# A two-dimensional FFT filter on one core: sequence length 2048 split 64 by 32 in place of 128 by 16

## The chip, the core and the metric

The kernel runs on one NeuronCore of a Trainium2 chip. TensorE (PE) multiplies matrices and writes PSUM. ScalarE (ACT) and VectorE (DVE) work on elements and copy PSUM to SBUF. GpSimd (POOL) and SyncE (SP) issue DMA transfers here, and 16 DMA engines carry them. The metric is the device time of one execution in microseconds; smaller is better.

## The reference

Two filters act on the same input x of 2048 rows (s) by 1024 columns (d), in bf16. Each multiplies the real 2-D spectrum by a complex weight, and a gate for each row blends the two results:

```python
def reference(A_x, A_w_r, A_w_i, B_x, B_w_r, B_w_i, gate_w):
    x = A_x
    g = sigmoid((x * gate_w).sum(-1, keepdims=True))
    a = irfft2(rfft2(x.astype(float32)) * (A_w_r + 1j * A_w_i), s=(2048, 1024)).astype(bfloat16)
    b = irfft2(rfft2(x.astype(float32)) * (B_w_r + 1j * B_w_i), s=(2048, 1024)).astype(bfloat16)
    return g * a + (1 - g) * b
```

The input B_x is not used.

## The kernel before

All transforms are matmuls with constant matrices (`make_constants`, lines 49 to 125). A row index is written s = 16 s2 + s1: s2 (128 values) lies on the SBUF partitions and s1 (16 values) along them. The transform over s is done in two steps, 128 by 16. The transform over d is split into even frequencies (`par` 0, with 257 columns) and odd ones (`par` 1, with 256). Frequencies of s come in 16 tiles t, and two tiles are a unit; there are 8 units for each parity, so n runs from 0 to 15, the even ones first.

1. First forward step (lines 214 to 228). For each s1, 8 matmuls with F1 contract s2 and fold d with d + 512; ScalarE and VectorE in turn copy the result into y.
2. Unit steps, for each n. f2 (8 matmuls with FD, L275, copy into T, L279) contracts d. f3 (12 matmuls of 64x64 tiles with WF, L295, in parity 0 also 8 of one column, L303; copy into X, L310) does the s1 step of the forward transform. cmul (four VectorE operations, L325 to L331) multiplies by the weights of A and B. i1 (two rounds r of 8 matmuls with WI, L344, copy into rl, L349) does the first inverse step over s. After the second round POOL issues the exchange (L354): the rows of rl, which have frequency and s1 on the partitions, go to RR[par], where 128 components of s2 lie on the partitions and s1 lies along them.
3. Output blocks, for each parity and v from 0 to 7, with two values of s1 in a block. i2 (L367, 16 pairs of weight load and matmul of 128 columns) contracts the 128 components of A with the tile EA and then those of B with EB, adding both in PSUM; ScalarE copies the result into V (L370). i3 (L378, 8 matmuls of 512 columns with IG) does the inverse over d. For parity 0 the result is kept in SBUF in fp32, copied by ScalarE for v below 3 (L384) and by VectorE after that (L386). For parity 1 VectorE forms the sum and the difference (L389, L390) and SP stores both halves of d.

The gate is computed from the same spectrum. `gate_hat` contracts y with the gate weight, ScalarE writes zs with single elements moved apart (L245), and a small transfer on ScalarE's queue (L246) puts one logit component on each partition (zt). `gate_z` (L254) multiplies zt, repeated over 128 columns, with Ez, so that the logit stands on every partition, and ScalarE applies the sigmoid (L256). `gate_weights(b)` forms EA = g E (L261) and EB = E - EA (L262) for four values of s1.

The order is written out by hand (lines 393 to 449) and every engine keeps it. Unit steps are staggered: in round n stand f2(n), i1(n-3, 0), f3(n-1), i1(n-3, 1), cmul(n-1). From n = 12 on, i2(0, v) and i3(0, v) stand between the unit steps of the odd parity: i2(0, 0) follows i1(9, 1). The last i2 of parity 0 and all of parity 1 follow the last unit. The PSUM pool pt has three buffers; the i2 result pv has one (`bufs=1`, L413), so an i2 waits for the copy of the one before it. The buffers rl are four: the copy for unit n + 4 waits for the exchange of unit n. RR[0] takes the place of x, RR[1] that of weight tiles, and the fp32 tile EV shares the bytes of RR[0]. POOL's transfers use eight completion semaphores in turn, so that in the built program each transfer also waits until the eighth one before it has landed. SP issues the loads of x, of the constants and of the weights in the order of lines 163 to 201, and the later weight loads from within the rounds.

Of the kernel before, what the change touches and what calls it, by code (L numbers as in the profile page):

```python
# [27 lines left out]

def quad_reps(t):
    return (0, 32, 16, 48) if t == 0 else (t, t + 32, t + 64, t + 96)  # L30


def half_k2(t, jh):
    a, b = quad_reps(t)[2 * jh:2 * jh + 2]
    if t == 0 and jh == 0:
        return (0, 64, 32, 96)
    return (a, 128 - a, b, 128 - b)


def half_rows(t, jh):  # L40
    return np.array([k2 + 128 * k1 for k2 in half_k2(t, jh) for k1 in range(16)])

# [6 lines left out]
def make_constants():  # L49
    c = {}  # L50
    s2 = np.arange(128)
    F = np.zeros((128, NT, 2, 2, 2))
    E = np.zeros((NT, 2, 2, 2, 128))
    EZ = np.zeros((NT, 2, 2, 2, 128))
    for t in range(NT):
        for j, k2 in enumerate(quad_reps(t)):
            th = 2 * np.pi * s2 * k2 / 128
            F[:, t, j // 2, 0, j % 2] = np.cos(th)
            F[:, t, j // 2, 1, j % 2] = -np.sin(th)
            E[t, j // 2, 0, j % 2] = np.cos(th)  # L60
            E[t, j // 2, 1, j % 2] = np.sin(th)
            EZ[t, j // 2, 0, j % 2] = 2 * np.cos(th)
            EZ[t, j // 2, 1, j % 2] = -2 * np.sin(th)
            if k2 == 0:
                F[:, t, j // 2, 1, j % 2] = np.cos(np.pi * s2)
                E[t, j // 2, 1, j % 2] = np.cos(np.pi * s2)
                EZ[t, j // 2, 0, j % 2] = 1
                EZ[t, j // 2, 1, j % 2] = np.cos(np.pi * s2)
# [24 lines left out]
    c["IG"] = _bf16np(IG.reshape(2, 2, 2, 128, 512).transpose(3, 0, 1, 2, 4).reshape(128, 8, 512))  # L93
    s1 = np.arange(NS1)
    WF = np.zeros((128, NT, 3, 64))
    WI = np.zeros((128, NT, 3, 64))
    for t in range(NT):
        for jh in range(2):
            k = half_rows(t, jh)
            reps = quad_reps(t)[2 * jh:2 * jh + 2]  # L100
            al = np.zeros((NS1, 2, 2, 64), dtype=complex)
            be = np.zeros((2, 2, NS1, 64), dtype=complex)
            for p in range(64):
                w = np.exp(-2j * np.pi * k[p] * s1 / S)
                kk = k[p] % 128
                if kk in (0, 64):
                    cc = 0 if kk == 0 else 1
                    al[:, cc, 0, p] = w
                    be[cc, 0, :, p] = w.conj()
                    continue  # L110
                eps = 1 if kk in reps else -1
                j = reps.index(kk if eps > 0 else 128 - kk)
                al[:, 0, j, p] = w
                al[:, 1, j, p] = 1j * eps * w
                be[0, j, :, p] = w.conj()
                be[1, j, :, p] = 1j * eps * w.conj()
            al = al.reshape(64, 64)
            be = be.reshape(64, 64).T
# [10 lines left out]
def gated_mix(ctx, tc, x_in, we_in, wo_in, gw_in, out):  # L129
# [99 lines left out]

    RR = [r[:].rearrange("p (s f) -> p s f", s=NS1) for r in (Re, Ro)]  # L230
# [16 lines left out]

    g = const.tile([P, NS1, 128], BF16, name="g")

    def gate_z():  # L250
        for hh in range(2):
            ps = ptile()
            for s in range(8):
                nc.tensor.matmul(ps[:, s * 128:(s + 1) * 128], lhsT=zt[:, 8 * hh + s:8 * hh + s + 1].to_broadcast([P, 128]),  # L254
                                 rhs=Ez[:], start=True, stop=True)
            nc.scalar.activation(g[:, 8 * hh:8 * hh + 8, :].rearrange("p a b -> p (a b)"), ps[:], ACT.Sigmoid)  # L256

    def gate_weights(b):
        s = slice(4 * b, 4 * b + 4)
        e = bc(Ec[:]).to_broadcast([P, 4, 128])  # L260
        nc.vector.tensor_tensor(EA[:, s], g[:, s], e, ALU.mult)  # L261
        nc.vector.tensor_tensor(EB[:, s], e, EA[:, s], ALU.subtract)  # L262

# [70 lines left out]
    def i1(n, r):  # L334
        par, u = n // NU, n % NU
        Y = Ys[n]
        o = 1 if par == 0 and r == 1 else 0
        ps = ptile()
        for k in range(2):
            w = ((0, 2), (1, 0))[r][k]  # L340
            for tt in range(2):
                for jh in range(2):
                    hin = hp(jh ^ tt)
                    nc.tensor.matmul(ps[hp(jh), tt * 512:(tt + 1) * 512], lhsT=WI[hin, 2 * u + tt, w, :],  # L344
                                     rhs=Y[hin, k, 2 * tt:2 * tt + 2, o:o + 256], start=(k == 0), stop=(k == 1))
        if r == 0:
            RLs[n] = wk.tile([P, 2, 2, 512], BF16, name="rl", tag="rl", bufs=4)
        rl = RLs[n]
        nc.scalar.copy(out=rl[:, :, r, :], in_=ps[:].rearrange("p (t m) -> p t m", t=2))  # L349
        if r == 1:  # L350
            for tt in range(2):
                t = 2 * u + tt
                p0 = 32 * (t // 4) + t % 4
                nc.gpsimd.dma_start(RR[par][p0:p0 + 29:4, :, :], rl[:, tt].rearrange("p r m -> p (r m)"))  # L354
            RLs.pop(n), Ys.pop(n)
# [3 lines left out]
    def i2(par, v):  # L359
        ps = pq["p"].tile([P, 1024], F32, name="pv", tag="pv")  # L360
        V = wk.tile([P, 2, 4, 128], BF16, name="V", tag="V")
        for s in range(2):
            s1 = 2 * v + s
            for ch in range(4):
                c0 = (ch // 2) * 512 + (ch % 2) * 128
                for ab, Ew in enumerate((EA, EB)):
                    nc.tensor.matmul(ps[:, s * 512 + ch * 128:s * 512 + ch * 128 + 128],  # L367
                                     lhsT=RR[par][:, s1, c0 + 256 * ab:c0 + 256 * ab + 128], rhs=Ew[:, s1, :],
                                     start=(ab == 0), stop=(ab == 1))
        nc.scalar.copy(out=V[:].rearrange("p s c k -> p (s c k)"), in_=ps[:])  # L370
        Vs[par, v] = V
# [115 lines left out]
```

## Time and profile before

| what | value |
|---|---|
| time, median of 3 runs | 147.13 us (145.34, 147.13, 148.02) |
| profiled execution: span from first to last instruction | 144.4 us |
| profiled execution: its own device time | not given apart from the span |
| PE busy | 121.9 us, 1188 matmuls |
| DVE busy | 97.6 us, 113 instructions |
| ACT busy | 93.3 us, 97 instructions |
| POOL busy | 19.6 us, of which 32 exchange issues 19.1 us |
| DMA | 29.19 MB in 11088 packets, mean 202 GB/s |
| exchange alone | 8.41 MB in 4608 packets on POOL's queue |
| granted TensorE clock, mean | 0.961 of full speed |

A PE that is busy is not one at its peak, since matmuls overlap in the pipeline and each record holds its whole passage: a matmul of 128 columns is recorded with 219 ns, but the next one starts 56 ns later. Starts tell the pace. In a chain view each piece has its start, its length and the work that the next piece waited for.

### The profile page before, as it was taken

How to read it: one execution, taken by the hardware profiler on the slowest of the kernel's cores; microseconds unless marked ns; L12 is line 12 of the kernel's file. 1: busy time of each engine (PE TensorE's matmuls, PEld its weight loads, DVE VectorE, ACT ScalarE, POOL GpSimd, SP SyncE). 2: the span in 40 equal slices, each digit the busy share in tenths (PEclk: the TensorE clock that was granted, in tenths of full speed). 3: DMA queues.
4: the chain of work that ended last, by engine and by line, in shares of the span. 5: the costliest groups of instructions: out<-in, count | busy, mean ns of one | idle time of the engine just before them, and what ended most of it. 6: DMA issues, size and time to landing. Idle time of an engine off the chain costs nothing.

```text
span 144.4 us, 2878 instructions
## 1 busy us (share of the span) xinstructions
PE 121.9 (84%) x1188; PEld 68.1 (47%) x1206; DVE 97.6 (68%) x113; ACT 93.3 (65%) x97; POOL 19.6 (14%) x37
## 2 busy tenths in 40 slices
PE   6999979929899898888867999868869999999910
PEld 2688844416344443334324345433455665756500
DVE  0177740089279999999999279599433456898990
ACT  4255546665699999999995899997935244253200
POOL 1000000000033222233333033033330000000000
PEclk9999999975799999999999999999999999999985
DMA  4999999968716999999865315527464000464553
GB/s 148 298 361 419 406 411 405 415 244 284 297 14 168 240 279 278 353 250 202 163 139 133 126 18 140 131 43 168 110 166 110 0 0 0 167 253 166 208 228 145
DMA packets 11088, 29.19 MB, mean 202 GB/s; under 512 B 3781, under 2 KB 4165, under 8 KB 10949
## 3 DMA queue, kind: packets, MB, share of 16 engines
q1 hardware_dynamic: 6048, 20.55, 38.3%
q0 software_dynamic: 4608, 8.41, 24.8%
q8 instruction: 9, 0.15, 0.5%
q10 hardware_dynamic: 420, 0.07, 0.3%
q14 instruction: 3, 0.02, 0.0%
HBM read 16.42 MB, written 4.19 MB: 143 GB/s over the span
## 4 chain that ended last, share of the span: by engine, by line
PE 55%; ACT 24%; DMA 9%; issue 4%; DVE 2%; another core or an unknown queue 2%; DVEq 1%; POOL 0%; ACTq 0%; POOLq 0%
PE pt L378 18%; PE pt L218 10%; PE pt L275 10%; ACT rl L349 10%; PE pv L367 9%; DMA re<-rl 5%; DMA zt<-zs 4%; ACT X L310 4%; ACT T L279 3%; PE pt L344 3%; ACT V L370 2%; PE pt L155 2%; ACT zs L245 2%; DVE ot L390 2%
## 5 line engine op out<-in xcount | busy, mean ns | idle before, releaser
L275 PE MATMUL pt<-fd,y 128*128 128x512 bf16 x117 | 30.5, 394 | 3.8 <-ACT rl L349 2.6
L349 ACT CAST rl<-pt 128x1024 bf16<-128x1024 f32 x32 | 32.9, 1038 | 0.0
L378 PE MATMUL pt<-ig,V 128*128 128x512 bf16 x121 | 29.6, 379 | 1.1 <-ACT V L370 0.7
L370 ACT CAST V<-pv 128x1024 bf16<-128x1024 f32 x16 | 16.3, 1021 | 19.2 <-PE pv L367 19.2
L344 PE MATMUL pt<-Y,wi 64*64 64x512 bf16 x256 | 20.1, 387 | 3.8 <-ACT T L279 0.8
L275 PEld LDWEIGHTS <-y 128*128 128x128 bf16 x128 | 12.6, 100 | 20.3 <-issue 8.6
L279 ACT CAST T<-pt 128x1024 bf16<-128x1024 f32 x16 | 16.3, 1017 | 8.3 <-PE pt L275 4.1
L378 PEld LDWEIGHTS <-V 128*128 128x128 bf16 x128 | 11.7, 98 | 13.9 <-ACT V L370 1.9
L354 POOL DMA_DIRECT2D re<-rl x16 | 9.6, 606 | 59.8 <-ACT rl L349 59.8
L310 ACT CAST X<-pt 128x1024 bf16<-128x1024 f32 x16 | 16.5, 1033 | 0.0
L218 PE MATMUL pt<-f_84,re 128*128 128x256 bf16 x128 | 15.6, 289 | 0.0
L218 PEld LDWEIGHTS <-re 128*128 128x128 bf16 x128 | 13.0, 103 | 3.1 <-DMA re<-in_x_dram 0.8
L228 ACT CAST y<-pt 128x1024 bf16<-128x1024 f32 x8 | 8.1, 1013 | 8.4 <-PE pt L218 8.4
L354 POOL DMA_DIRECT2D ro<-rl x16 | 9.5, 596 | 26.4 <-ACT rl L349 26.4
L386 DVE COPY re<-pt 128x1024 f32<-128x1024 f32 x5 | 6.1, 1225 | 10.2 <-PE pt L378 10.2
L226 DVE CAST y<-pt 128x1024 bf16<-128x1024 f32 x7 | 8.6, 1225 | 5.2 <-PE pt L218 5.2
L344 PEld LDWEIGHTS <-wi 64*64 64x64 bf16 x256 | 6.4, 106 | 11.9 <-issue 10.7
L389 DVE TENSOR_TENSOR ot<-pt,re 128x1024 bf16<-128x1024 f32 x8 | 9.8, 1224 | 3.0 <-PE pt L378 3.0
L367 PE MATMUL pv<-ea,re 128*128 128x128 bf16 x64 | 8.1, 219 | 2.9 <-DMA re<-rl 1.7
L295 PE MATMUL pt<-T,wf 64*64 64x512 bf16 (+2 forms) x192 | 9.8, 307 | 0.4 <-ACT T L279 0.3
L367 PEld LDWEIGHTS <-re 128*128 128x128 bf16 x128 | 7.5, 98 | 5.4 <-issue 2.5
L390 DVE TENSOR_TENSOR ot<-re,pt 128x1024 bf16<-128x1024 f32 x8 | 9.7, 1210 | 0.0
(96 smaller groups left out, 128.2 us busy)
## 6 DMA issues: line engine op xcount, KB each, us to landing
re<-rl POOLq DMA_DIRECT2D x16, 256.0 KB, 8.0
ro<-rl POOLq DMA_DIRECT2D x16, 256.0 KB, 5.1
out_dram<-ot SPq DMA_DIRECT2D x8, 512.0 KB, 2.6
re<-in_x_dram SPq DMA_DIRECT2D x7, 512.0 KB, 8.6
ro<-in_we_dram SPq DMA_DIRECT2D x4, 516.0 KB, 8.0
y<-in_wo_dram SPq DMA_DIRECT2D x4, 512.0 KB, 6.5
fd<-cst_fd SPq DMA_DIRECT2D x2, 512.0 KB, 9.1
ig<-cst_ig SPq DMA_DIRECT2D x1, 1024.0 KB
```

What stands on the lines that cost most here:

```text
L218: nc.tensor.matmul(ps[:, q * 256:(q + 1) * 256], lhsT=x[:, s1, h * 512 + q * 128:h * 512 + (q + 1) * 128], rhs=(bc(F1[:, 0, :]).to_broadca ...
L275: nc.tensor.matmul(ps[:, tt * 512:(tt + 1) * 512], lhsT=y[:, q, par, 2 * t:2 * t + 2, :, :].rearrange("p j s c -> p (j s c)"), rhs=FD[:, p ...
L279: nc.scalar.copy(out=T[:].rearrange("p a b -> p (a b)"), in_=ps[:])
L295: nc.tensor.matmul(ps[ho, tt * 512 + dst:tt * 512 + dst + ln], lhsT=WF[hp(jh), 2 * u + tt, w, :], rhs=T[hp(jh), tt, src:src + ln], start=( ...
L310: nc.scalar.copy(out=xo, in_=ps[:].rearrange("p (t r m) -> p t r m", t=2, r=2))
L344: nc.tensor.matmul(ps[hp(jh), tt * 512:(tt + 1) * 512], lhsT=WI[hin, 2 * u + tt, w, :], rhs=Y[hin, k, 2 * tt:2 * tt + 2, o:o + 256], start ...
L349: nc.scalar.copy(out=rl[:, :, r, :], in_=ps[:].rearrange("p (t m) -> p t m", t=2))
L354: nc.gpsimd.dma_start(RR[par][p0:p0 + 29:4, :, :], rl[:, tt].rearrange("p r m -> p (r m)"))
L367: nc.tensor.matmul(ps[:, s * 512 + ch * 128:s * 512 + ch * 128 + 128], lhsT=RR[par][:, s1, c0 + 256 * ab:c0 + 256 * ab + 128], rhs=Ew[:, s ...
L370: nc.scalar.copy(out=V[:].rearrange("p s c k -> p (s c k)"), in_=ps[:])
L378: nc.tensor.matmul(ps[:, s * 512:(s + 1) * 512], lhsT=V[:, s, ch, :], rhs=IG[:, par * 4 + ch, :], start=(ch == 0), stop=(ch == 3))
L390: nc.vector.tensor_tensor(ot[:, :, 1, :], ev, pv, ALU.subtract)
```

## The change

A row index is now split 64 by 32. The partitions still hold s2 = 0 to 127 with s = 16 s2 + s1, but the matrices read s2 as 2 p + h: p (64 values) is the long part, and s1 + 16 h (32 values) the short one. A tile's 128 rows are now four frequencies of 64 with 32 steps each, where they were eight of 128 with 16.

- The A and B components, 64 each, lie together on the 128 partitions of RR: A on 0 to 63, B on 64 to 127. One matmul contracts both, with a single tile EG: E times sigmoid(z) on partitions 0 to 63 and E times sigmoid(-z) on 64 to 127. The sign is a scale operand (sgn, two POOL memsets) of the sigmoid. i2 keeps 16 matmuls, each now with 64 columns and no accumulation.
- `gate_weights` is one VectorE operation on 8 x 64 elements in place of two on 4 x 128; EA and EB are one tile EG.
- The copy into V puts the two halves h next to each other: it reads PSUM in order and writes with a step of two elements.
- The exchange of a unit is four transfers, one for each tile and each of A and B: 4 partitions of 32 pieces of 1 KB, where two transfers had 8 partitions of 16 pieces of 2 KB. The copy into rl writes runs of 256 elements, not 512.
- `gate_z` has 32 matmuls of 64 rows and 64 columns in place of 16 of 128 and 128. Ez and Ec are smaller, and zt has 64 partitions of 32 elements instead of 128 of 16.

Everything else stays, the number of matmuls in the other stages and the written order included. In the changed file the lines stand some 6 lines earlier: the exchange is at L348, i2's matmul at L361, the copy into rl at L344.

```diff
-    Ec = const.tile([P, 128], BF16, name="ec")
-    Ez = const.tile([P, 128], BF16, name="ez")
+    Ec = const.tile([P, 64], BF16, name="ec")
+    Ez = const.tile([64, 64], BF16, name="ez")
...
-    EA = const.tile([P, NS1, 128], BF16, name="ea")
-    EB = const.tile([P, NS1, 128], BF16, name="eb")
-    zt = const.tile([P, NS1], BF16, name="zt")
+    EG = const.tile([P, 32, 64], BF16, name="eg")
+    zt = const.tile([64, 32], BF16, name="zt")
+    sgn = const.tile([P, 1], F32, name="sgn")
+    nc.gpsimd.memset(sgn[0:64], 1.0)
+    nc.gpsimd.memset(sgn[64:128], -1.0)
...
-            for s in range(8):
-                nc.tensor.matmul(ps[:, s * 128:(s + 1) * 128], lhsT=zt[:, 8 * hh + s:8 * hh + s + 1].to_broadcast([P, 128]),
+            for i in range(16):
+                w, sp = divmod(16 * hh + i, 2)
+                s1 = w + 16 * sp
+                nc.tensor.matmul(ps[:, i * 64:(i + 1) * 64], lhsT=zt[:, s1:s1 + 1].to_broadcast([64, 128]),
                                  rhs=Ez[:], start=True, stop=True)
-            nc.scalar.activation(g[:, 8 * hh:8 * hh + 8, :].rearrange("p a b -> p (a b)"), ps[:], ACT.Sigmoid)
+            nc.scalar.activation(g[:, 16 * hh:16 * hh + 16, :].rearrange("p a b -> p (a b)"), ps[:], ACT.Sigmoid, scale=sgn[:])
...
     def gate_weights(b):
-        s = slice(4 * b, 4 * b + 4)
-        e = bc(Ec[:]).to_broadcast([P, 4, 128])
-        nc.vector.tensor_tensor(EA[:, s], g[:, s], e, ALU.mult)
-        nc.vector.tensor_tensor(EB[:, s], e, EA[:, s], ALU.subtract)
+        s = slice(8 * b, 8 * b + 8)
+        nc.vector.tensor_tensor(EG[:, s], g[:, s], bc(Ec[:]).to_broadcast([P, 8, 64]), ALU.mult)
...
-            RLs[n] = wk.tile([P, 2, 2, 512], BF16, name="rl", tag="rl", bufs=4)
+            RLs[n] = wk.tile([P, 4, 2, 256], BF16, name="rl", tag="rl", bufs=4)
         rl = RLs[n]
-        nc.scalar.copy(out=rl[:, :, r, :], in_=ps[:].rearrange("p (t m) -> p t m", t=2))
+        nc.scalar.copy(out=rl[:, :, r, :], in_=ps[:].rearrange("p (t m) -> p t m", t=4))
         if r == 1:
-            for tt in range(2):
-                t = 2 * u + tt
-                p0 = 32 * (t // 4) + t % 4
-                nc.gpsimd.dma_start(RR[par][p0:p0 + 29:4, :, :], rl[:, tt].rearrange("p r m -> p (r m)"))
+            for ta in range(4):
+                p0 = 64 * (ta % 2) + 16 * (ta // 2) + u % 4 + 32 * (u // 4)
+                nc.gpsimd.dma_start(RR[par][p0:p0 + 13:4, :, :], rl[:, ta].rearrange("p r m -> p (r m)"))
...
         for s in range(2):
-            s1 = 2 * v + s
             for ch in range(4):
-                c0 = (ch // 2) * 512 + (ch % 2) * 128
-                for ab, Ew in enumerate((EA, EB)):
-                    nc.tensor.matmul(ps[:, s * 512 + ch * 128:s * 512 + ch * 128 + 128],
-                                     lhsT=RR[par][:, s1, c0 + 256 * ab:c0 + 256 * ab + 128], rhs=Ew[:, s1, :],
-                                     start=(ab == 0), stop=(ab == 1))
-        nc.scalar.copy(out=V[:].rearrange("p s c k -> p (s c k)"), in_=ps[:])
+                for sp in range(2):
+                    k = 4 * v + 2 * s + sp
+                    nc.tensor.matmul(ps[:, s * 512 + ch * 128 + sp * 64:s * 512 + ch * 128 + sp * 64 + 64],
+                                     lhsT=RR[par][:, k, ch * 128:ch * 128 + 128], rhs=EG[:, k, :], start=True, stop=True)
+        nc.scalar.copy(out=V[:].rearrange("p s c (k e) -> p (s c) e k", e=2), in_=ps[:].rearrange("p (a e k) -> p a e k", e=2, k=64))
```

Left out of the diff are the new contents of the constant matrices (F1, E, EZ, WF, WI), which change in value and not in the work that they cost, and RR's view as 32 by 512.

More of the change, by code (lines that the diff above doesn't have):

```diff
@@ L26, in _bf16np, with comp_row @@
     return np.ascontiguousarray(np.asarray(a, dtype=np.float32).astype(ml_dtypes.bfloat16))
-def quad_reps(t):
-    return (0, 32, 16, 48) if t == 0 else (t, t + 32, t + 64, t + 96)
 def half_k2(t, jh):
[L34 to L37, printed above, removed]
+    b = 2 * t + jh
+    return (0, 32) if b == 0 else (b, 64 - b)
 def half_rows(t, jh):
-    return np.array([k2 + 128 * k1 for k2 in half_k2(t, jh) for k1 in range(16)])
+    return np.array([k2 + 64 * k1 for k2 in half_k2(t, jh) for k1 in range(32)])
+def comp_row(ab, b, cc):
+    t, jh = b // 2, b % 2
+    u, tt = t // 2, t % 2
+    return 64 * ab + 16 * tt + 4 * (2 * jh + cc) + u % 4 + 32 * (u // 4)
 def unit_rows(t):
@@ L50, in make_constants @@
     c = {}
[L51 to L68, printed above, removed]
+    s2 = np.arange(64)
+    F = np.zeros((64, 2, 32, 2, 2))
+    E = np.zeros((128, 64))
+    EZ = np.zeros((32, 2, 64))
+    for b in range(32):
+        th = 2 * np.pi * s2 * b / 64
+        f = [np.cos(th), -np.sin(th)]
+        e = [np.cos(th), np.sin(th)]
+        ez = [2 * np.cos(th), -2 * np.sin(th)]
+        if b == 0:
+            f[1] = e[1] = ez[1] = np.cos(np.pi * s2)
+            ez[0] = np.ones(64)
+        for cc in range(2):
+            EZ[b, cc] = ez[cc]
+            for h in range(2):
+                F[:, h, b, cc, h] = f[cc]
+                E[comp_row(h, b, cc)] = e[cc]
     F = F.reshape(128, 128)
     c["F1"] = _bf16np(np.concatenate([F, -F], axis=1))
-    c["E"] = _bf16np(E.reshape(4, 4, 8, 128).transpose(0, 2, 1, 3).reshape(128, 128))
-    c["EZ"] = _bf16np(EZ.reshape(128, 128) / 128)
+    c["E"] = _bf16np(E)
+    c["EZ"] = _bf16np(EZ.reshape(64, 64) / 64)
     d1 = np.arange(512)
@@ L93, in make_constants @@
     c["IG"] = _bf16np(IG.reshape(2, 2, 2, 128, 512).transpose(3, 0, 1, 2, 4).reshape(128, 8, 512))
-    s1 = np.arange(NS1)
+    s1 = np.arange(32)
+    pos = np.array([w + 16 * sp for w in range(16) for sp in range(2)])
     WF = np.zeros((128, NT, 3, 64))
@@ L99, in make_constants @@
             k = half_rows(t, jh)
[L100 to L118, printed above, removed]
+            w = np.exp(-2j * np.pi * np.outer(s1, k) / S)
+            al = np.zeros((2, 32, 64), dtype=complex)
+            if t == 0 and jh == 0:
+                al[0, :, :32] = w[:, :32]
+                al[1, :, 32:] = w[:, 32:]
+                be = al.conj()
+            else:
+                eps = np.where(np.arange(64) < 32, 1, -1)
+                al[0], al[1] = w, 1j * eps * w
+                be = np.stack([w.conj(), 1j * eps * w.conj()])
+            al = al.reshape(2, 2, 16, 64).transpose(2, 0, 1, 3).reshape(64, 64)
+            be = be[:, pos].reshape(64, 64).T
             h = slice(64 * jh, 64 * jh + 64)
@@ L228, in gated_mix @@
             nc.scalar.copy(out=yo[:, :, s1, :], in_=i_)
[L230 removed]
+    RR = [r[:].rearrange("p (s f) -> p s f", s=32) for r in (Re, Ro)]
     EV = Re[:].bitcast(F32).rearrange("p (s f) -> p s f", s=NS1)
[L232 to L234 removed]
+    EG = const.tile([P, 32, 64], BF16, name="eg")
[3 more added lines that the diff above has]
+    nc.gpsimd.memset(sgn[64:128], -1.0)
     def gate_hat():
@@ L246, in gate_hat @@
         nc.scalar.dma_start(zt[:], zs[0:97:32].rearrange("p t c s -> p (t c s)"))
-    g = const.tile([P, NS1, 128], BF16, name="g")
+    g = const.tile([P, 32, 64], BF16, name="g")
     def gate_z():
```

## The prediction

> **What bounds the kernel now.** I read four views in this order: the busy time by stretches, the chain of work that ended last, single groups and stretches of the timeline where the chain passes an edited line, and the exchange transfers. The first says which engine limits each stage.
>
> ```profile
> core 0: us, PE busy (x) PEld busy (x) DVE busy (x) ACT busy (x) POOL busy (x), PEclk, DMA share, GB/s
> 0.80:37.50 36.70, 32.03 (x255) 20.59 (x262) 17.58 (x22) 19.14 (x19) 0.25 (x1) 0.91 0.93 348
> 37.50:74.90 37.40, 32.96 (x395) 15.10 (x400) 33.17 (x41) 35.57 (x38) 10.81 (x18) 1.00 0.83 214
> 74.90:104.90 30.00, 25.46 (x260) 12.37 (x266) 22.00 (x30) 26.41 (x29) 7.10 (x12) 1.00 0.44 108
> 104.90:120.30 15.40, 14.14 (x138) 9.41 (x139) 6.12 (x5) 6.08 (x7) 1.18 (x2) 1.00 0.24 64
> 120.30:144.40 24.10, 17.33 (x150) 10.62 (x150) 18.72 (x16) 6.07 (x6) 0.00 (x0) 0.91 0.43 175
> ```
>
> After the first columns (stretch, its length) stand the busy times. Until 37.5 us loads fill the DMA engines (0.93). From 37.5 to 74.9 ScalarE is full (35.57 of 37.40). From 74.9 to 104.9 ScalarE and TensorE alternate. From 104.9 TensorE carries the end, with VectorE close behind from 120.3.
>
> ```profile
> 69.90 6.53 DMA re<-rl
> ...
> 76.57 1.13 PE pv L367 x16
> ...
> 112.48 0.89 PE pv L367 x16
> 113.38 1.73 PE pt L378 x8
> ```
>
> In the chain (start, length, work) the last exchange transfer of the even half lands at 76.43 and releases the first i2 at 76.57. Later i2 (L367, 0.89) and i3 (L378, 1.73) alternate with no gap: one output block costs 2.62 us.
>
> ```profile
> 75.77 0.42 DVE L261 TENSOR_TENSOR ea<-g,ec 128x512 bf16<-128x512 bf16 x1
> 76.22 0.42 DVE L262 TENSOR_TENSOR eb<-ec,ea 128x512 bf16<-128x512 bf16 x1
> ...
> 136.10 1.23 DVE L389 TENSOR_TENSOR ot<-pt,re 128x1024 bf16<-128x1024 f32 x1 [0.27 <-PE pt L378]
> 137.24 1.21 DVE L390 TENSOR_TENSOR ot<-re,pt 128x1024 bf16<-128x1024 f32 x1
> 138.37 1.22 DVE L389 TENSOR_TENSOR ot<-pt,re 128x1024 bf16<-128x1024 f32 x1
> ```
>
> VectorE finishes the first gate tiles at 76.64, 0.2 us after that transfer: two waits end together at the first i2. At the end a pair of output operations needs 138.37 - 136.10 = 2.27 us, so VectorE has 0.35 us of air in each 2.62.
>
> ```profile
> L354 POOL DMA_DIRECT2D re<-rl x16: 596/596/745, 41.6 to 69.9; - x16
> DMA to landing us min/median/max: 4.5/8.0/12.0
> ```
>
> An issue costs POOL 0.596 us; even-half transfers landed 4.5 to 12.0 us after issue. The odd half's, with fewer loads beside them, took 4.3 to 5.7, median 5.1.
>
> **The change part by part.** *Second inverse stage, TensorE.* Each i2 keeps 16 load-and-matmul pairs but streams 64 columns in place of 128. Rows: 16 matmuls of 128 columns in 0.89 us are 56 ns each, 8 of 512 columns in 1.73 are 216; so a column costs (216 - 56) / 384 = 0.417 ns and a matmul 2.6 more. With 64 columns: 29 ns, or 0.47 us an i2, a gain of 0.42. This holds if the weight load, whose size stays 128x128, fits in 29 ns.
>
> ```profile
> 29.62 0.23 PE L303 MATMUL pl<-T,wf 64*64 64x1 bf16 x8 [0.49 <-DVE X L313]
> ...
> 79.91 0.11 PEld L378 LDWEIGHTS <-V 128*128 128x128 bf16 x2 [0.41 <-issue]
> ```
>
> Two full loads took 0.11 us together at 98 ns each, so the second began some 12 ns after the first; and 8 one-column pairs took 0.23 us, one alone 0.167, so pairs can follow each other at 9 ns. Bounds for a pair are 29 ns (columns alone) and 56 ns (nothing gained); I take 29, the side of these rows.
>
> [...]
>
> Where the 0.42 lies on the path: (a) First i2, start to end 76.57 to 77.53: next paragraphs. (b) Second, at 86.51: TensorE leads there, but ScalarE idles only 0.33 us waiting for it (before L384 at 91.73), so 0.33. (c) Third and fourth: V's copy waits for ScalarE, busy from 94.45 to 99.2 and 100.2 to 104.9; nothing. (d) i2(0,4) to i2(0,7), i2(1,0), i2(1,1): TensorE is the chain: 6 x 0.42 = 2.5. (e) The last six: a block would cost TensorE 0.47 + 1.73 = 2.20, but VectorE needs 2.27 and becomes the limit. The eight L389 starts now run from 120.38 to 138.37, 17.99 us; seven gaps of 2.27 are 15.9: gain 2.1.
>
> *Gate tiles.* Four VectorE operations of 0.45 (start to start) go. Three lie ahead of idle VectorE time (3.49, 1.66 and 2.36 us) or of work ScalarE holds back, worth nothing. The first matters: one tile is ready at 76.2 where the second was at 76.64.
>
> *Exchange.* A unit's two transfers of 256 KB become four of 128 KB, rows of 1 KB in place of 2. POOL issues 64 in place of 32: 2.4 us a unit in a pitch of 3.96 (65.35 to 69.31), so POOL has room; nothing else queues there. The last even unit's fourth issue begins at 69.31 + 3 x 0.596 = 71.1. Landing after 4.3 (quickest odd transfer) gives 75.4, after 5.1 gives 76.2, after 6.53 (today's last) 77.6. One wait is added: a transfer waits for the eighth before it on POOL; that reached four units back and now two. Unit 5 landed at 72.14 in the trace; an issue held until then lands 5.1 to 6.5 later, 77.2 to 78.7. Behind it stand unit 8's transfers and, by rl's four buffers, copies L349, whose margin was small (unit 3 landed at 66.04, the copy into its buffer began at 66.17). I take 76.2, the typical row, since with few loads left the units resemble the odd ones; both ends go to the range. With the gate at 76.2 the first i2 ends at 76.67, not 77.53: gain 0.86. ScalarE had 0.80 and 0.77 us of idle time before its next two copies, so it follows.
>
> [...]
>
> *V's copy (L370)* now writes bf16 with a step of two elements. L228 writes runs of four elements 128 B apart in 1,013 ns, no slower than a contiguous copy; L245 writes single elements 32 B apart: 512 in 2,343 ns, against 592 for 512 in L224. V's step of 4 B is far nearer to the first; I take 1.02, no change, and keep 4 x 1.02 = 4.1 as the other end.
>
> *Gate logits.* 32 matmuls of 64 columns replace 16 of 128: the same 2,048 columns, 16 more starts at 2.6 ns doubled at half clock, +0.1 (upper end +1.7, were each held at today's (1.89 - 0.31) / 15 = 105 ns); the transfer of zt has 64 rows, not 128, of a packet phase of 1.3 us (30.3 to 31.6): -0.1, between 0 and -0.6. The sigmoid's sign operand and two small POOL memsets (98 ns row) sit ahead of 2.38 us of ScalarE idle: 0. Copy L349 gets runs of 256, as L310 has (1,033 against 1,038): 0. SP issues as many transfers as before, two of them smaller: 0.
>
> Sum: -0.86 - 0.33 - 2.5 - 2.1 + 0.1 - 0.1 = -5.8 us. The profiled span of 144.4 becomes 138.6. The profile gives no other time for that execution; the runs lie 0.9 to 3.6 above the span, their median 2.7. Keeping that distance, 147.13 - 5.8 = 141.3.
>
> **The rivals.** *A: loads bound i2.* If a pair stays at 56 ns, only the earlier first i2 remains (0.4): 146.7. Against it: the 12 ns between loads. For it: no row shows 128-column loads with matmuls under 56 ns.
>
> *B: the exchange lands late.* With the window of eight, the first i2 waits until 78.7, 2.5 later than forecast. TensorE would idle 3.8 us, and in slices 9 to 11 the page shows what such thin stretches cost: granted clock 7, 5, 7 tenths, and 8 matmuls of f2 in 3.19 us where 1.89 is usual. I add 2 us for one such phase: 141.3 + 4.5 = 145.8. For it: landings of 8 to 12 us among the loads. Against it: the loads end at 64.6, and each transfer is half as large. It turns to a loss beyond a landing at 76.2 + 5.8 = 82, less the clock's part.
>
> *C, slower: V's copy.* At 4.1 us each, the first four cost ScalarE 4 x 3.1 = 12 more; in the rest the single pv buffer makes a block 0.72 + 4.1 + 0.05 = 4.9, twelve blocks some 27 over 2.62. About 184. It decides from about 1.75 us a copy, where 4 x 0.73 + 12 x 0.27 eats the 5.8. For it: L245. Against it: L228.
>
> **How the numbers follow.** Forecast 0.58 (139.5 to 143.5 by itself: the fastest run less 5.8, and 141.3 with some landing delay); A 0.09; B 0.21; C 0.08; unnamed losses 0.04. Two per cent, about what a measurement here can tell, is 2.9 us: faster is below 144.2, slower above 150.1. Faster: forecast and the milder 0.05 of B, 0.63. Same: A and 0.12 of B, 0.21. Slower: C, 0.04 of B and the unnamed, 0.16. The range from 138.5 to 147.2 takes in A and most of B; C, B's far end, the unnamed and 0.02 below stay out, 0.18.
>
> **What would show it.** Right: 16 L361 matmuls in about 0.47 us; output pairs 2.27 apart with VectorE never waiting; V's copy near 1.02; first i2 near 76.2, released by VectorE. Wrong: pairs at 56 ns; a DMA wait before the first i2 beyond 1.7 us or a lower PEclk after it; idle ScalarE time before the rl copies; V's copy over 1.7. The forecast fails most easily at the landing of the last even unit.

## The result, and the profile after

The changed kernel takes 152.81 us in the median of 4 runs (151.63 to 153.31), the kernel before beside it 146.44 (145.34 to 148.02): a ratio of 1.0448, 95% interval 1.0357 to 1.0538. It is slower, where 141.3 was forecast with a range of 138.5 to 147.2. The profiled execution took 152.97, with a span of 150.8. All ratios here leave out runs more than 1.5% above the fastest of their kernel, medians are over all runs, and the profiles of E1, E3, E4, E9 and E15 are of such longer runs.

The busy time by stretches, kernel after, for two of the stretches shown of before, with the same columns (the last three are the granted TensorE clock, the share of the DMA engines and GB/s):

```profile
37.50:74.90 37.40, 28.92 (x323) 13.02 (x328) 28.52 (x36) 29.86 (x32) 19.59 (x29) 0.95 0.71 183
...
104.90:120.30 15.40, 11.38 (x118) 5.45 (x122) 6.94 (x10) 10.49 (x10) 9.37 (x14) 0.89 0.51 116
```

The first of them tells it: ScalarE, full before (35.57 of 37.40), now works 29.86, and no other engine is full. All wait for something that is no engine. The DMA engines are not full either (0.71, before 0.83), so their mean shows no lack of bytes a second. The chain of waits of after names it (start, length, work):

```profile
45.13 12.01 DMA re<-rl
...
57.42 0.68 POOL re L348
58.10 12.13 DMA re<-rl
...
70.52 0.46 POOL re L348
...
73.24 7.60 DMA re<-rl
81.13 3.00 DMA ro<-rl
...
84.15 1.01 PE pv L360 x16
...
107.67 2.77 PE pt L370 x6
...
115.56 0.48 PE pv L360 x16
```

A transfer of unit 1 lands 12.01 us after its issue. That landing releases POOL's issue of the eighth transfer after it, in unit 3. The next transfer of unit 3 lands 12.13 us after its issue and releases unit 5. The last even transfer is issued at 77.43 and lands at 84.01, and the first i2 starts at 84.15. (The last row of this wait is named ro<-rl because a part of an odd transfer happened to finish at the same moment.) The row at 107.67 shows six matmuls of i3 in 2.77 us, where eight take 1.73: TensorE ran at half clock there (granted clock 0.50 from 107.67 to 110.44, 0.81 from 106 to 115 us; before 1.00).

The groups and waits of after that belong to it:

```profile
L348 POOL DMA_DIRECT2D re<-rl x32: 688/691/820, 40.5 to 77.4; - x32
...
  POOL re L348: 7.7, 8
...
  ACT rl L344: 4.6, 2
...
DMA to landing us min/median/max: 3.9/6.7/14.9
```

This is the view of the transfers' line: the median issue costs POOL 0.691 us, and the last even one starts at 77.4 (before: 69.9). Among those who waited for these transfers (us, times) stand POOL itself and ScalarE's copy into rl. A landing, the time from issue to arrival, took up to 14.9 us. ScalarE's copy into V, first before, then after:

```profile
L370 ACT CAST V<-pv 128x1024 bf16<-128x1024 f32 x16 | 16.3, 1021 | 19.2 <-PE pv L367 19.2
```

```profile
L362 ACT CAST V<-pv 128x1024 bf16<-128x1024 f32 x16 | 21.0, 1312 | 13.9 <-PE pv L360 13.9
```

V's copy takes 1.312 us, not 1.02. And the end of the kernel, first the chain, then VectorE's timeline:

```profile
126.68 0.47 PE pv L360 x16
127.14 1.73 PE pt L370 x8
```

```profile
135.70 1.21 DVE L381 TENSOR_TENSOR ot<-pt,re 128x1024 bf16<-128x1024 f32 x1
136.84 1.21 DVE L382 TENSOR_TENSOR ot<-re,pt 128x1024 bf16<-128x1024 f32 x1
137.96 1.21 DVE L381 TENSOR_TENSOR ot<-pt,re 128x1024 bf16<-128x1024 f32 x1
```

Here the change does what it was said to do: i2 in 0.47 us, output pairs 137.96 - 135.70 = 2.26 apart.

Cut at two events that the chain shows in both kernels, the first i2 and i2(0,4):

| stage | before | after | difference |
|---|---|---|---|
| start to first i2 | 76.57 | 84.15 | +7.6 |
| first i2 to i2(0,4) | 28.5 | 31.4 | +2.9 |
| i2(0,4) to the end of the span | 39.4 | 35.2 | -4.1 |
| span | 144.4 | 150.8 | +6.4 |

### The profile page after: what moved, and what is told of

Read it like the earlier page. It is cut to its first block, busy times and chain, and to the rows that moved or that the text cites. A ratio compares the mean times of both kernels' runs of the same rounds, so it can differ in the third digit from the quotient of the medians.

```text
span 150.8 us, 2955 instructions
## 1 busy us (share of the span) xinstructions
PE 117.6 (78%) x1204; PEld 61.7 (41%) x1222; DVE 95.3 (63%) x109; ACT 98.2 (65%) x97; POOL 44.6 (30%) x71
## 4 chain that ended last, share of the span: by engine, by line
DMA 33%; PE 31%; ACT 16%; DVE 7%; issue 5%; POOL 3%; DVEq 1%; SPq 1%; another core or an unknown queue 0%; ACTq 0%
DMA re<-rl 21%; PE pt L370 12%; PE pt L211 8%; ACT rl L344 5%; DVE ot L382 5%; DMA ro<-rl 5%; PE pt L270 5%; DMA zt<-zs 4%; PE pv L360 4%; DMA re<-in_x_dram 3%; ACT X L305 3%; ACT V L362 3%; POOL re L348 2%; DVE ot L381 2%; ACT T L274 2%
## 5 line engine op out<-in xcount | busy, mean ns | idle before, releaser
L270 PE MATMUL pt<-fd,y 128*128 128x512 bf16 x117 | 32.3, 409 | 8.9 <-ACT rl L344 7.3
L348 POOL DMA_DIRECT2D re<-rl x32 | 22.1, 694 | 54.8 <-ACT rl L344 42.7
L344 ACT CAST rl<-pt 128x1024 bf16<-128x1024 f32 x32 | 32.8, 1035 | 4.6 <-DMA re<-rl 4.6
L370 PE MATMUL pt<-ig,V 128*128 128x512 bf16 x121 | 30.9, 392 | 2.6 <-ACT V L362 2.1
L362 ACT CAST V<-pv 128x1024 bf16<-128x1024 f32 x16 | 21.0, 1312 | 13.9 <-PE pv L360 13.9
L348 POOL DMA_DIRECT2D ro<-rl x32 | 21.9, 689 | 18.4 <-ACT rl L344 16.4
L339 PE MATMUL pt<-Y,wi 64*64 64x512 bf16 x256 | 20.2, 388 | 3.9 <-DVE Y L325 1.1
L320 DVE TENSOR_TENSOR p<-X,w 128x2056 bf16<-128x2056 bf16 (+1 forms) x16 | 19.0, 1226 | 6.2 <-ACT X L305 6.1
L305 ACT CAST X<-pt 128x1024 bf16<-128x1024 f32 x16 | 16.5, 1030 | 0.0
L320 DVE TENSOR_TENSOR p<-X,y 128x2048 bf16<-128x2048 bf16 x8 | 9.4, 1219 | 9.5 <-ACT X L305 9.5
L211 PE MATMUL pt<-f,re 128*128 128x256 bf16 x128 | 14.6, 276 | 0.7 <-DMA re<-in_x_dram 0.4
L211 PEld LDWEIGHTS <-re 128*128 128x128 bf16 x128 | 12.6, 99 | 3.3 <-DMA re<-in_x_dram 1.7
L378 DVE COPY re<-pt 128x1024 f32<-128x1024 f32 x5 | 6.1, 1225 | 11.5 <-PE pt L370 11.5
L325 DVE TENSOR_TENSOR Y<-p,p 128x1028 bf16<-128x1028 bf16 (+1 forms) x16 | 11.1, 696 | 1.1
L326 DVE TENSOR_TENSOR Y<-p,p 128x1028 bf16<-128x1028 bf16 (+1 forms) x16 | 11.0, 688 | 0.0
## 6 DMA issues: line engine op xcount, KB each, us to landing
y<-in_wo_dram SPq DMA_DIRECT2D x4, 512.0 KB, 12.2
```

The costliest lines, as they stand in the source:

```text
L211: nc.tensor.matmul(ps[:, q * 256:(q + 1) * 256], lhsT=x[:, s1, h * 512 + q * 128:h * 512 + (q + 1) * 128], rhs=(bc(F1[:, 0, :]).to_broadca ...
L270: nc.tensor.matmul(ps[:, tt * 512:(tt + 1) * 512], lhsT=y[:, q, par, 2 * t:2 * t + 2, :, :].rearrange("p j s c -> p (j s c)"), rhs=FD[:, p ...
L305: nc.scalar.copy(out=xo, in_=ps[:].rearrange("p (t r m) -> p t r m", t=2, r=2))
L320: nc.vector.tensor_tensor(p[:, :, :, 0:M], xb, w[:, :, :, 0:M], ALU.mult)
L325: nc.vector.tensor_tensor(Y[:, 0, :, 0:M], p1[:, :, 0, 0:M], p2[:, :, 1, 0:M], ALU.subtract)
L348: nc.gpsimd.dma_start(RR[par][p0:p0 + 13:4, :, :], rl[:, ta].rearrange("p r m -> p (r m)"))
```

## The experiments

What can make the exchange late? *Theory 1*: the number of transfers, four a unit against the eight that POOL may have under way. *Theory 2*: rows of 1 KB. *Theory 3*: four destination partitions a transfer in place of eight. *Theory 4*: the loads beside them. Each of the first three is a part of the change that the kernel before can be given alone.

**E1, E2, E3: the kernel before with four transfers a unit, cut in three ways**

```
E1  + for so in range(2): dma_start(RR[par][p0:p0+29:4, so::2, :], rl[so::2, tt])
E2  + for jh in range(2): dma_start(RR[par][p0+16*jh:p0+16*jh+13:4, :, :], rl[64*jh:64*jh+64, tt])
E3  + for q in range(2):  dma_start(RR[par][p0:p0+29:4, :, 512*q:512*q+512], rl[:, tt, q])
```

> The kernel before, with each exchange transfer cut into two by even and odd s1: four transfers a unit, still 8 destination partitions, 2 KB rows and the same bytes; nothing else differs. Theory 1 (the number of transfers: POOL may have eight under way, so four a unit leave only two units open, and each start waits for a landing 10 to 12 us long while the loads run): the last even transfer lands near 82 to 85 instead of 76.4, the first i2 goes from 76.57 to 82 to 85, and the time by 5 to 8 us, to 151 to 155. Theory 2 (rows of 1 KB) and theory 3 (four destination partitions a transfer): nothing of either is here, so the first i2 stays at 76 to 78 and the time within 1.5 us of the kernel before.

> The kernel before, with each exchange transfer cut into two by the halves of the source's partitions: four transfers a unit, each from 64 partitions to 4, 2 KB rows, same bytes. Theory 1 (number of transfers against the window of eight): first i2 at 82 to 85, time 151 to 155, as with the cut by s1. [...] Theory 2 (1 KB rows): unchanged, within 1.5 us of the kernel before.

> The kernel before, with each exchange transfer cut into two by r: four transfers a unit to 8 partitions, and rows of 1 KB in place of 2 KB, twice as many rows, same bytes. Theory 1 (number of transfers): first i2 at 82 to 85, time 151 to 155, like the other two cuts. Theory 2 (1 KB rows): this cut alone is slow, 151 to 155, and the other two are not. Theory 3 (4 destination partitions): unchanged, within 1.5 us of the kernel before.

E1: 145.80 (143.96 to 146.85, 10 runs), ratio 0.9939 (0.9885 to 0.9993). E3: 145.30 (143.21 to 147.67), 0.9926 (0.9863 to 0.9989). Neither costs anything: the number alone and the rows alone fall. E2, the only one of the three that theory 3 had slow (151 to 155), has a ratio of 1.0022 (0.9961 to 1.0083), with a median over all ten runs of 149.35, spread from 146.08 to 152.53. Five of the ten took 150.2 or more, nearly as long as the changed kernel, but the profile is of the shortest, so E2's time decides nothing. Its landings do. The rows of the even half's transfers of E1 and of E2 (KB each, median us to landing):

```profile
re<-rl POOLq DMA_DIRECT2D x32, 128.0 KB, 5.4
```

```profile
re<-rl POOLq DMA_DIRECT2D x32, 128.0 KB, 8.0
```

Same number, same bytes, same 2 KB rows: with 8 partitions the even half lands in 5.4 us, with 4 in 8.0 (E3: 5.1; after: 7.8); the odd half in 3.1 and 4.5. And the waits of POOL on its own transfers, E2:

```profile
POOL re L355 <- DMA re<-rl: 9.2, 11, 1.9
```

It was 2.3 us in 3 waits in E1 and none in the kernel before. So the window of eight closes where transfers land late, and in the kernel before it is the four partitions that make them later. In E2's profiled execution the units 5 to 7 caught up (first i2 at 76.43); the changed kernel does not. Beyond four partitions it has 1 KB rows, which cost nothing with eight partitions (E3), and 0.69 us an issue where E2 has 0.62; no run tells which of the two keeps it from catching up.

**E4: half of the changed kernel's transfers on SP's queue**

```
- nc.gpsimd.dma_start(RR[par][p0:p0 + 13:4, :, :], ...)
+ (nc.gpsimd, nc.sync)[ta % 2].dma_start(RR[par][p0:p0 + 13:4, :, :], ...)
```

> The changed kernel, with two of the four transfers of each unit issued from SP's queue in place of POOL's; rows, partitions and bytes as in the changed kernel. POOL then has two transfers a unit, as before the change. Theory 1 (window of eight): the window no longer holds POOL back, the last even transfer lands at 76 to 79, the first i2 starts 5 to 8 us earlier than 84.15, and the time falls to 144 to 148. Theories 2 and 3 (rows of 1 KB, 4 partitions a transfer) and theory 4 (DMA engines shared with the loads make every part late): the landings stay near 10 to 12 us beside the loads, the first i2 stays at 82 to 86, and the time at 151 to 154.

161.32 us (159.84 to 164.92), ratio 1.0927 (1.0821 to 1.1034): outside what any theory expected. POOL did not wait for its own transfers any more, but SP's, which share their queue with the weight loads, were the slower ones. The chain of E4:

```profile
73.69 15.61 DMA re<-rl
...
89.96 1.01 PE pv L360 x16
```

The trace notes the completion of a transfer in 16 counts. In the first transfer of a quiet odd unit, the changed kernel's (issued at 93.34) has 12 of them within 2.56 us and 4 at 3.29 to 4.39, that of the kernel before (84.98) 8 within 2.54 and 8 at 3.65 to 4.54. Which engines served a transfer no run shows. The 15.61 us include SP's own instruction (0.55 to 6.57 us in the even half, median 1.20), and how much of the rest is due to the loads ahead in SP's queue was not tested.

**E5: eight partitions in the changed kernel**

```
- p0 = 64 * (ta % 2) + 16 * (ta // 2) + u % 4 + 32 * (u // 4)
- ... RR[par][p0:p0 + 13:4, :, :]
+ p0 = 32 * (u // 2) + 2 * (u % 2) + ta // 2;  h = 16 * (ta % 2)
+ ... RR[par][p0:p0 + 29:4, h:h + 16, :]
```

> The changed kernel, with each exchange transfer laid out over 8 destination partitions of 16 rows in place of 4 of 32: still four transfers a unit, 128 KB each, 1 KB rows, issued by POOL; all of re and ro is filled, but the values stand in other places than the computation needs, so the output is other numbers. [...] Theory 5 (four partitions are not it; the changed kernel's exchange is late for another reason, such as 0.69 us an issue or what the other engines do at the time): landings stay near 8, the first i2 at 82 to 86, the time at 150 to 154.

143.53 us (141.22 to 144.31), ratio 0.9894 (0.9783 to 1.0005), against 1.0448 with four partitions: the loss is gone, though a gain over the kernel before is not shown. The profiled execution took 141.22, span 139.2. Its even half's transfers, and its first i2 in the chain:

```profile
re<-rl POOLq DMA_DIRECT2D x32, 128.0 KB, 5.3
```

```profile
70.56 3.10 DMA ro<-rl
...
73.69 0.63 PE pv L361 x16
```

Theory 3 expected landings of 3 to 6 us here, the first i2 at 75 to 78 and a time of 141 to 146; the first i2 came earlier still. It holds, and theory 5 falls: four transfers a unit, 1 KB rows and a window of two units are all still there, and the first i2 starts 10.5 us earlier. Two things come along with the eight partitions. An issue takes 0.596 us again in place of 0.69; a link of after's chain holds one or two issues beside a landing of 12 us, so this should be worth under 1 us by itself (an estimate). And the first i2 here needs only half of the positions: it starts at 73.69, while the last even transfer lands at 74.06. (The row 70.56 is named ro<-rl as in after; the last transfer that i2 needs landed at 73.56.)

**E6: more buffers for rl**

```
- RLs[n] = wk.tile(..., tag="rl", bufs=4)
+ RLs[n] = wk.tile(..., tag="rl", bufs=6)
```

> The changed kernel with six buffers for rl in place of four. If the exchange is late because POOL waits for the landing of the transfer eight places before (theory 1 with 3), the buffers only move ScalarE's waits: the last even transfer still lands at 83 to 85, the first i2 stays at 83 to 85, and the time within 1.5 us of the changed kernel's 152. Rival: the buffers are the cause (ScalarE's copy into rl waited up to 4.2 us for a transfer, and TensorE behind it): the first i2 starts at 78 to 81 and the time is 147 to 149.

151.23 us (150.72 to 151.44), ratio 1.0401 (1.0323 to 1.0478); first i2 at 82.50. ScalarE's wait for a buffer is gone (4.6 us in after, none here), and the time hardly moves: the buffers pass the lag on, they don't make it. One of its links in E6:

```profile
56.75 11.42 DMA re<-rl
```

**E7: without the odd half's loads**

```
-     nc.sync.dma_start(w, w_in[par][u])
+     if n < 8:
+         nc.sync.dma_start(w, w_in[par][u])
```

> The changed kernel without the eight loads of the odd half's weights (units 8 to 15, 4 MB between 38 and 66 us): the odd half multiplies by what the buffers held, so the output is other numbers. Theory 4 (the exchange is late because its parts share the DMA engines with these loads): landings of the even half fall to 4 to 7 us, POOL does not wait, the first i2 starts at 75 to 79, and the time is 142 to 147. If the loads do not matter (four partitions and eight places alone are slow enough): landings of 7 to 12 us remain, first i2 at 82 to 85, time 150 to 153.

143.67 us (142.81 to 144.41), ratio 0.9884 (0.9795 to 0.9972). The line's own view, E7:

```profile
  POOL re L349: 1.8, 1
...
DMA to landing us min/median/max: 4.0/6.6/8.1
```

No landing over 8.1 us, one wait of POOL in the even half, first i2 at 76.17. So the lag needs both: four partitions and the loads beside them. Four partitions alone give 6.6 us, and two units start about 8 us apart, so the window of eight is wide enough. E7 also shows that 0.69 us an issue does not make the lag where the loads are missing.

**E8: V written contiguously**

```
- nc.scalar.copy(out=V[:].rearrange("p s c (k e) -> p (s c) e k", e=2), ...)
+ nc.scalar.copy(out=V[:].rearrange("p s c k -> p (s c k)"), in_=ps[:])
```

> The changed kernel with V written contiguously, in the order of PSUM, in place of 4 bytes apart: the rows of the output then stand in another order. The V copy should take 1.02 us again instead of 1.31 us. If ScalarE is on the path from the first i2 to i2(0,4), where four of these copies lie, the time falls by about 1.2 us, to 151 or so (150.5 to 152); if the copies are hidden there too, it stays within 0.5 us of the changed kernel's 152.3. The exchange is the same, so the first i2 stays at 83 to 85 in both.

151.88 us (149.83 to 154.36), ratio 1.0359 (1.021 to 1.0509); the copy took 1.020. Too wide a spread to tell 0.5 us from 1.2. In the profiles the stretch from the first to the fifth V copy falls from 30.9 us (after) to 29.9; before it was 28.3. The first i2 started at 81.51, outside the expected 83 to 85 though the exchange is the same: so much it varies from one execution to another.

**E9 to E12: the loads in other places**

```
E9   - 8 <= n < 12: load_w(n + 4)  into y        + n == 11: load_w(12); n == 12: load_w(13..15)  into wt[(n + 2) % 4]
E10  as E9, and  - 1 <= n < 5: load_w(n + 7)     + load_w(8), load_w(9) into Ro right behind load_w(7); n in (3, 4): load_w(n + 7)
E11  as E10, and V contiguous, with  + for e in range(2): dma_start(ov[e::2, ...], ot[64*e:64*e+64])
E12  the kernel before with E10's loads
```

> The changed kernel, with the weights of units 12 to 15 (2 MB) loaded later: into the buffers of units 10, 11, 8 and 9, so that the first of them waits for unit 10's products (near 78 us) in place of starting between 50 and 60 us. Output as in the reference. If the loads between 50 and 66 us are what makes the four-partition transfers land at 11 to 15 us (theory 4): the first i2 starts at 77 to 80 and the time is 144 to 148. If the earlier loads (units 8 to 11, from 38 to 52 us) start the lag by themselves: first i2 at 82 to 85, time 150 to 153.

> As the kernel with late loads of units 12 to 15, and the loads of units 8 and 9 moved ahead, into room in ro that is free until the odd half's exchange, right behind the first eight loads: two loads (units 10 and 11) are left beside the even half's exchange in place of eight. Output as in the reference. By theory 4 with 3 it should come near the run without any of these loads (143.7): first i2 at 75.5 to 78.5, time 142 to 146. If the late loads now hold up unit 12's products, a wait of VectorE for a load shows near 84 us and the time is 146 to 149.

> As the kernel with early and late loads, with V written contiguously (1.02 us a copy in place of 1.31) and the output's rows set right by two output transfers of 64 partitions a block in place of one of 128. Output as in the reference. If the V copies lie on the path in the middle stage: 0.5 to 1.5 us less than the kernel with early and late loads, so 141 to 145; if hidden, the same within 0.5 us; if two output transfers a block are slower than one, the end after the last sum grows by up to 1 us.

> The kernel before, with the same early and late loads: what the loads' places are worth by themselves. In the kernel before only the last unit's transfers (6.5 us, after the loads) release the first i2, so if the loads matter through POOL's window of two units alone, the first i2 stays at 75.5 to 77 and the time within 1 us of the kernel before. Rival: the loads cost the kernel before as well (its transfers took up to 12 us beside them): first i2 1 to 2 us earlier, time 143.5 to 145.

Medians 146.67 (142.93 to 149.70), 146.94 (145.99 to 148.10), 147.84 (144.96 to 149.10) and 146.10 (145.26 to 147.15), beside 146.61 for the kernel before; with four runs each, spread like this, no ratio is on record. The even half is nearly mended: the first i2 starts at 77.22, 78.13 and 76.56, and the medians lie 5.0 to 6.1 us below the changed kernel's 152.81. In the control E12 the first i2 starts at 75.05, 1.5 us earlier than before, as its rival expected, but the median is only 0.5 us below the kernel before: what the loads' places are worth there is not settled, and it is small beside 5 to 6 us. E9's time came as theory 4 expected; E10 and E11 stayed 1 to 3 us above their ranges. E10 has no wait of VectorE for a load near 84 us, the sign that its second expectation named. Its chain shows a wait in the odd half instead:

```profile
110.66 6.82 DMA ro<-rl
...
117.72 0.63 PE pv L360 x16
```

The last odd transfer is issued at 110.66 and takes 6.82; i2(1,0) waits for it until 117.72. Before, the odd half's last transfer landed at 111.43, 3.5 us ahead of i2(1,0). This wait is the smaller part: from the fifth V copy to i2(1,0) E10 takes 8.7 us where E5 takes 7.9. The larger part lies ahead of it: the first i2 is 1.9 us behind the forecast's 76.2, and the stretch between the first and the fifth V copy is 30.2 us, 1.9 more than before.

**E13, E14: eight partitions with every value in its place.** i1 forms its rows in tiles of 32 partitions, so that 128 rows hold 8 components of 16 positions, and a unit leaves in two transfers again. (The constant matrices, reordered to match, are left out below.)

```
- nc.tensor.matmul(ps[hp(jh), tt*512:(tt+1)*512], lhsT=WI[hin, 2*u+tt, w, :], ...)
+ q = 32 * (2 * tt + jh)
+ for sp in range(2):
+     nc.tensor.matmul(ps[q:q+32, sp*512:(sp+1)*512], lhsT=WI[hin, 2*u+tt, w, 32*sp:32*sp+32], ...)
  ...
+ nc.gpsimd.dma_start(RR[par][p0:p0 + 29:4, :, :], rl[:, ab]...)     # two a unit
```

> The changed kernel, with i1's output laid over 32-partition tiles: 16 matmuls of 32 columns in place of 8 of 64 for each half unit, so that the 128 rows hold 8 components of 16 positions, and a unit leaves in 2 transfers of 256 KB to 8 partitions with 2 KB rows, as in the kernel before. Output as in the reference. If theory 3 holds and TensorE runs the 32-column matmuls side by side (i1 costs no more in all): first i2 at 74 to 77, i2(1,0) near 113, time 140.5 to 143.5. Rival: the 16 matmuls cost twice the time of 8 (i1's 20 us becomes 40): TensorE becomes the bound of the unit rounds, first i2 at 80 to 86, time 148 to 155. If the exchange was not the failed step: time stays at 150 to 153 even with i1 unchanged in cost.

> As the kernel with i1 in 32-column matmuls, with V written contiguously and the output's rows set right by two output transfers a block. Output as in the reference. The V copy at 1.02 us in place of 1.31 should take 0.5 to 1.5 us off the stage between the first i2 and i2(0,4), so 139.5 to 142.5 where the other comes at 140.5 to 143.5; if those copies are hidden there, within 0.5 us of it; two smaller output transfers may give back up to 0.5 us at the end.

E13: 146.54 us (146.10 to 147.65, 12 runs), ratio 1.0046 (1.0009 to 1.0082). E14: 147.26 (144.95 to 148.50), 1.0103 (1.0037 to 1.0169). The view of E13's transfer line, its group of i1, and its second stretch:

```profile
  PEld L363: 0.4, 1
...
DMA to landing us min/median/max: 4.1/5.1/8.2
```

```profile
L341 PE MATMUL pt<-Y,wi 64*32 64x512 bf16 x512 | 33.6, 379 | 0.7 <-DVE Y L325 0.7
```

```profile
37.50:74.90 37.40, 37.40 (x490) 15.46 (x483) 31.14 (x39) 32.68 (x35) 9.66 (x16) 1.00 0.68 208
```

The exchange's waits are gone (0.4 us in all). The price is TensorE: i1 is busy 33.6 us where it was 20.2, and TensorE works 37.40 of 37.40 us. So of the 9.3 us between after and E5 the same change with a sound exchange gets back 6.3; the other 3.0 fit TensorE's 13 us more in i1, which no run separates further. E13 lies between its two expectations, above the 140.5 to 143.5 of theory 3. E14 also missed its 139.5 to 142.5, and its shorter V copies save nothing in the end: from the start of VectorE's last output operation to the end of the span, with two output transfers a block, it takes 6.9 us where E13 takes 5.3, against the 0.5 us that were allowed for it.

**E15 to E18: the interleaving in PSUM, and eight partitions in a few units**

```
E15  - ps[:, s*512 + ch*128 + sp*64 : ... + 64]      + ps[:, s*512 + ch*128 + sp : s*512 + ch*128 + 128 : 2]     (out of i2)
E16  E13 and E15
E17  E10 and E15, with E13's i1 and transfers in units 6 and 7
E18  the same in units 5, 6, 7, 14 and 15
```

> The changed kernel, with the rows interleaved by the second inverse stage's matmuls (every other column of PSUM) in place of by ScalarE's copy, so V is read and written contiguously; output as in the reference. Exchange as in the changed kernel: first i2 at 82 to 85. V copy 1.02 us in place of 1.31. If 4 to 8 of these copies lie on the path from the first i2 to i2(0,4), the time is 1.2 to 2.4 us below the changed kernel's 152.3: 149.5 to 151.5. If TensorE's writes to every other column cost it as much, its matmuls rise from 193 ns and the time stays at 152 to 153.

> The kernel with i1 in 32-column matmuls for all units (8 partitions a transfer, 2 transfers a unit), with the interleaving in TensorE's writes to PSUM and one output transfer a block. Output as in the reference. Against 146.5 for it with the copy that interleaves: 1 to 2.5 us less, 143.5 to 146, as TensorE's 13 us more in i1 stay.

> The changed kernel with the early and late loads, the interleaving in TensorE's writes, and 32-column i1 with 8-partition transfers in units 6 and 7 alone, whose transfers release the first i2. Output as in the reference. By theory 3 the last even transfers land 4 to 5 us after their issue in place of 6.3 and are issued 1.4 us sooner: first i2 at 75 to 77, time 142 to 145. If the units before (still 4 partitions) keep POOL back, first i2 at 77 to 79 and the time 144 to 147.

> As the kernel before it in this list, with 8-partition transfers in units 5, 6, 7, 14 and 15. Output as in the reference. If the odd half's last transfers hold i2(1,0) as well (it started at 118.4 where the 8-partition run with values in other places had 113.2), the time falls by 0.5 to 2 us more, to 141 to 144; if TensorE pays as much for the three further units (0.8 us each), the same within 0.7 us.

E15 153.45 us, ratio 1.0425 (1.0280 to 1.0570); E16 152.68, 1.0460 (1.0364 to 1.0557); E17 148.47 (145.04 to 155.20), no ratio; E18 146.86, 1.0019 (0.9961 to 1.0077). E15 shows why none gains. Groups and chain of E15:

```profile
L362 ACT CAST V<-pv 128x1024 bf16<-128x1024 f32 x16 | 16.3, 1021 | 20.1 <-PE pv L360 20.1
...
L360 PE MATMUL pv<-eg,ro 128*128 128x64 bf16 x128 | 8.5, 245 | 0.0
```

```profile
124.97 0.89 PE pv L360 x16
125.86 1.73 PE pt L370 x8
```

V's copy is back at 1.021 us, but an i2 whose results go to every other column of PSUM takes 0.89 us, as with 128 columns: the whole gain of the second stage is gone, and a block costs 2.62 again. E16 to E18 carry the same loss, 16 x 0.42 = 6.7 us of TensorE, and all miss their expectations. E16 lies 6.1 above E13, close to that loss; how much of the miss of E17 and E18 is due to it was not measured apart. What they show of the exchange: in E17, with eight partitions in units 6 and 7 alone, the first i2 starts at 75.47 and i2(0,4)'s copy at 104.84 (after: 116.11). A kernel that interleaves in PSUM before i2(0,4), where ScalarE is scarce, and in ScalarE's copy behind it was not tried; no variant of the changed kernel with the reference's output beat the kernel before.

## Why the prediction was wrong

*i2, right.* Pairs at 29 ns, an i2 in 0.47 us. The end of 56 ns was not reached.

*The end, right.* Blocks 2.26 apart (forecast 2.27), VectorE the limit. The two terms of 2.5 and 2.1 make 4.6; 4.1 was measured. The eight output pairs came as forecast (starts from 128.9 to 144.8, 15.9 us); the stretch ahead of them gained 2.0, not 2.5.

*Exchange, the step that failed.* It said "I take 76.2, the typical row, since with few loads left the units resemble the odd ones", with 78.7 as the far end. Measured: 84.15. The sum had the last issue at 71.1, with no wait, and its landing 5.1 us later; the issue began at 77.43 and landed 6.58 later. So 6.3 of the 8 us are POOL's late issue, 1.5 the landing itself. Three parts of the step failed. First, the landing: the last even unit's four transfers took 6.6 to 7.9 us, not 4.3 to 6.5, since a transfer half as large with four partitions lands later, not earlier (E1 against E2: 5.4 and 8.0; E5: 5.3). Second, and the largest, the wait on the eighth before was worked out from unit 5's landing in the trace of before, as if the units ahead landed as they did then; the chain of after runs through units 1, 3 and 5, each held by the one two before, at 12 us a step. A wait that feeds itself is not bounded by one link of it. Third, POOL's issue: 0.69 us, not 0.596, and 0.596 again in E5, which has 8 partitions of 16 rows in place of 4 of 32.

*Rival B named this mechanism* and put 145.8 on it, 4.5 us above the forecast, where 11.5 came. Its price was too small by the chain above, and its threshold, a loss beyond a landing at 82 less the clock's part, was too late: E8 and E6, with the first i2 at 81.51 and 82.50, are already 3.6 and 4.0% slower than the kernel before, and E10, at 78.13, shows no gain (146.94 beside 146.61). Its chance of 0.21 leaned on "each transfer is half as large". The granted clock fell as it said (0.94 from 74.9 to 104.9 and 0.89 from 104.9 to 120.3, where before had 1.00).

*V's copy, mis-sized.* 1.02 was taken, 1.31 measured: 0.29 more, four times before i2(0,4), some 1.2 us (E8 got 1.0 of it back). Rival C had the direction; 1.75 us, where it would decide, is far.

*The stage from the first i2 to i2(0,4), mis-sized too.* The sum had it 0.8 us shorter than before (27.6, by 76.2 and 105.03 less 0.86 and 0.33); it took 31.4. Of these 3.8 us V's copies make about 1. On the chain six matmuls of f2 took 1.97 us (before 1.46) and six of i3 2.77 (about 1.3 at the pace of the others), together some 2 us of lower clock, an estimate. So of the 12.2 us between the forecast span of 138.6 and the measured 150.8, 8.0 arise before the first i2, 3.8 in this stage and 0.5 behind it.

*First i2, -0.86: not tested cleanly.* Whether an earlier first i2 shortens the kernel before depends on the execution. E12 started it 1.52 us earlier (75.05), and its fifth V copy came 1.19 earlier (104.83 against 106.02). E1 started it 2.15 us earlier (74.42), and its fifth V copy came only 0.13 earlier (105.89), but in E1 the granted clock was 0.94 from 74.9 to 104.9 us, where E12 and the kernel before had 1.00.

*The agreement of E5 with the forecast is partly luck.* Its profiled span of 139.2 lies near the forecast 138.6, but that is its fastest run, and its first i2 started at 73.69, 2.5 us ahead of the forecast, while the stage behind it took longer than forecast. The median of its runs, 143.53, is 2.2 us above 141.3: with a sound exchange too, the forecast was too low.

*Gate logits*: 1.58 us (before 1.89), landing of zt 5.66 (before 5.80): -0.3 and -0.1 where +0.1 and -0.1 were forecast. Small, as the prediction said, though one sign was wrong.

*The exchange of a quiet odd unit*: 5.7 us from first issue to last landing before (84.98 to 90.70) and 7.2 after (93.34 to 100.56). Most of the difference is POOL's issuing: the last issue starts 0.59 us after the first before and 2.04 after, and from the last issue to the last landing it is 5.13 before and 5.18 after.

Open: why four partitions suffer so much more from the loads than eight, with the same bytes in all. In after, one of the 16 completion counts of a transfer comes 1.9 to 3.7 us behind the one before it in seven of the eight transfers of units 1 and 2 (landings 10.5 to 15.0 us); the trace doesn't say why.

## What to carry to other kernels

When a layout changes, look at how many partitions each transfer still reaches, not at its bytes: fewer partitions made transfers of the same size land later (E1 5.4 us, E2 8.0), and beside other loads so late that the queue stood still (up to 14.9 in after, 8.1 in E7 without those loads). Where a queue may have a fixed number of transfers under way, eight here, splitting them shortens its reach, here from four units to two; follow that wait through the whole chain with the landing time of the loaded stretch, not by one link from the old trace. When one variant seems to confirm the rest of a forecast, check stage by stage whether two misses have cancelled.

## What the runs showed of the hardware

- 128x128 weight loads with 64-column matmuls follow each other at 29 ns (16 in 0.47 us, after); with results to every other PSUM column at 56 (0.89, E15).
- Matmuls of 64x32 tiles with 512 columns came at 61 ns each (16 in 0.98 us, E13), those of 64x64 at 70 (8 in 0.56, after): half the output rows, nearly the same time.
- ScalarE's copy of 1,024 elements to bf16 with a step of 4 bytes: 1.31 us (after), contiguous 1.02 (before).
- An issue on POOL: 0.562 us for 8 partitions of 8 rows (E1), 0.596 for 8 of 16 (before, E3, E5), 0.622 for 4 of 16 (E2), 0.69 for 4 of 32 (after).
- E4, two of a unit's four transfers of 4 partitions on SP's queue: 15.6 and 16.5 us to land in the chain, SP's own instruction included (0.55 to 6.57 us in the even half), and up to 12.3 for POOL's beside them.
